# A leftover item's tokens gathered on GpSimd, one register-addressed copy a token

## The chip, the cores and the metric

The kernel runs on one core of one Trainium2 chip. The metric is the device time of one execution in microseconds, as the median over several runs; less is better. A core has five engines that run side by side and wait for each other by semaphores: TensorE (PE, matrix products; PEld is its loading of weights), VectorE (DVE), ScalarE (ACT), GpSimd (POOL) and SyncE (SP, which mostly issues DMAs). Each engine takes its own instructions in order.

## What is computed

Sigmoid attention, then two mixture-of-experts layers. Each of the 1792 tokens (4 batches of 448) has 768 numbers, each layer has 8 experts with 1024 hidden units, and a token uses one expert. Cut to what matters:

```python
x = attention(q, k, v)                                  # 1792 x 768
# layer 1: only tokens with x @ w_skip > 0, the others stay as they are
e_idx = argmax(x @ w_gate, axis=1)
x = x + gate_w * (relu(x @ w1[e_idx]) @ w2[e_idx])      # per token, its own expert
# layer 2: every token
e_idx = argmax(cosine(x, expert_emb) / tau, axis=1)
out = gate_w * (relu(x @ w1[e_idx]) @ w2[e_idx])
```

Everything is in float32. All the weights that are needed come from HBM at run time, since the routing depends on the data.

## The kernel before

The attention takes the first 160 us or so and leaves x transposed in SBUF, as `xT` (128 partitions, 6 chunks of 128 features, 1792 tokens). Most tokens of a batch go to one and the same expert, the primary one. So the kernel computes that expert for the whole batch of 448 tokens (`dense`), and the few tokens that go elsewhere are collected as **items**: an item is up to 64 tokens of one batch that go to one other expert. With these inputs one item is computed in each layer: the first (m = 0) beside the second dense block of layer 1, the other (m = 1) beside the last dense block of layer 2.

`dense` runs over 8 blocks f of 128 hidden units. On TensorE `h(f)` is 18 matmuls (6 chunks, each in three terms of split precision), then come 18 matmuls of `y(f - 1)`; for f = 0 there is no `y` ahead, so `h(0)` is followed directly by `h(1)`. After `h(f)` ACT and DVE evacuate the bank to `hh` and `hl`. Between these pieces are 16 slots, `sub(0)` to `sub(15)`: `sub(2f)` follows `h(f)`, `sub(2f + 1)` follows `y(f - 1)`. A slot emits the work that is hung on it, and since the schedule is manual (`tc.manual_schedule`), that is the order on each engine's queue. In even slots, `units` splits the next weights into a rounded part (ACT) and a remainder (DVE, `split_unit`). In the last block of layer 2, slot 0 first emits `pend`: 24 transposes, the scaling and the store of the output rows of the batch before (`finish`).

What an item hangs on the slots is written in `Item.ready` and `schedule`:

- `regs` loads the item's batch, expert and rank into registers of ACT, DVE and SP; `copy` copies the batch's 6 chunks of `xT` to `STG` (`xT[..., batch]` is addressed by register); both in slot k0, which is 3 for the first item and 1 for the other.
- `select`, four slots later, builds on DVE the selecting matrix `SEL` (token by place in the item, one where they match) and `GRC` (gate and token number).
- `turn(d)`, six of them, transposes a chunk of `STG` to rows in `ROW`, four transposes each, evacuated by ACT.
- `gather` multiplies `SEL` with `ROW` (8 products with 384 columns), `gatherT` turns the gathered rows back with three transposes, into `XB`, which lies in a free part of `ROW`.
- `gate` gathers gates and token numbers by products with `SEL`, and in the first item also transposes `SEL`.
- `first` and `second` fetch the expert's weights into the buffers of the raw weights; `h(s)`, `hT(s)` and `y(s)` compute the item in two halves, `h(0)` in slot 12, `h(1)` in 14; `y` comes after the dense block, in `finish`.
- `put` adds the result into `xT` (first item) or writes its rows to the output by an indirect DMA on GpSimd (the other).

GpSimd otherwise has nothing to do between 38 us and the end.

PSUM banks for this side work come from `bank()`, which alternates between two; dense `h(f)` uses the same two.

Of the kernel before, what the change touches and what calls it, by code (L numbers as in the profile page):

```python
# [12 lines left out]
I32 = mybir.dt.int32  # L13
# [8 lines left out]
def sigmoid_attention_moe_moe_kernel(  # L22
# [645 lines left out]
    def batch_cols(p, b):  # L668
        return xT[:, p, :].rearrange("q (b s) -> q b s", s=S)[:, ds(b, 1), :].rearrange("q o s -> q (o s)")
# [74 lines left out]
    ROW = wp.tile([128, C * DM], F32, tag="row", name="row")  # L744
    SELT = wp.tile([128, S], F32R, tag="selT", name="selT")
    SEL = wp.tile([128, 4 * 128], F32, tag="sel", name="sel")
    XB = ROW[:, 3 * DM : 3 * DM + ND * TL].rearrange("p (c t) -> p c t", t=TL)
    SMALL = wp.tile([128, 16], F32, tag="small", name="small")
    POSC, GS, IDX = SMALL[:P, 0:C], SMALL[:, 12:14], SMALL[:, 14:15].bitcast(I32)
    GRC = SMALL[:P, 4:12].rearrange("p (c t) -> p c t", t=2)  # L750
# [105 lines left out]
    class Item:  # L856


        def __init__(self, m, i):
            self.m, self.i = m, i  # L860
            self.wa, self.wb, self.R = (w1, w2, R1) if m == 0 else (v1, v2, R2)

        def regs(self):
            L, i, xe = self.R.LI, self.i, [ENG.Activation, ENG.DVE]
# [18 lines left out]
                    self.wb[ds(self.e, 1), u * 256 : (u + 1) * 256, :].rearrange("o (g p) d -> p (o g) d", p=128),  # L883
                )

        def copy(self):
            for d in range(ND):
                o = STG[:, d * S : (d + 1) * S]
                if d % 2:
                    nc.vector.tensor_copy(o, batch_cols(d, self.b))  # L890
                else:
                    nc.scalar.activation(o, batch_cols(d, self.b), AF.Copy)

        def select(self):
            R, j = self.R, self.j
            nc.vector.tensor_single_scalar(
# [15 lines left out]
                self.R.LI[0:1, ds(self.i + NL, 1)], engines=[ENG.DVE], min_val=0, max_val=NE - 1  # L912
            )

        def turn(self, d):


            def f():
                ps = bank("ps_xn")
                for c in range(C):  # L920
                    o = d * S + c * P
                    nc.tensor.transpose(ps[:P, c * 128 : (c + 1) * 128], STG[:, o : o + P], ident)
                o = ROW[:P].rearrange("p (c d) -> p c d", c=C)[:, :, d * 128 : (d + 1) * 128]
                nc.scalar.activation(o, ps[:P, :].rearrange("p (c d) -> p c d", c=C), AF.Copy)

            return f

        def gather(self):

            hw = DM // 2  # L930
            ps = bank("ps_xg")
            for c in range(C):
                for g in range(2):
                    nc.tensor.matmul(
                        ps[TL * g : TL * g + TL, :hw], lhsT=SEL[:P, c * 128 : c * 128 + TL],
                        rhs=ROW[:P, c * DM + g * hw : c * DM + g * hw + hw], start=c == 0, stop=c == C - 1,
                    )
            self.xg = spare()
            nc.scalar.activation(self.xg[:, :hw], ps[:, :hw], AF.Copy)

        def gatherT(self):
            ps = bank("ps_xs")
            for i in range(3):
                nc.tensor.transpose(ps[:, i * 128 : i * 128 + 128], self.xg[:, i * 128 : i * 128 + 128], ident)
            nc.scalar.activation(
                XB.rearrange("p (g i) t -> p i g t", g=2), ps[:, :384].rearrange("p (i g t) -> p i g t", i=3, g=2), AF.Copy
            )

        def gate(self):
            ps = bank("ps_gs")  # L950
# [10 lines left out]
        def h(self, s):  # L961


            def f():
                ps = bank("ps_h2")
                for c in range(ND):
                    for g in range(2):
                        nc.tensor.matmul(
                            ps[TL * g : TL * g + TL, :256], lhsT=XB[:, c, :],
                            rhs=as1(QUART[2 * s + g])[:, c, :], start=c == 0, stop=c == ND - 1,  # L970
                        )
                hs = self.hs = spare()
                nc.scalar.activation(hs[:, :256], ps[:, :256], AF.Relu)

            return f
# [37 lines left out]

        def ready(self, k0):

            prep = [self.turn(d) for d in range(ND)] + [self.gather, self.gatherT, self.gate]
            at = merge({k0: [self.regs, self.copy], k0 + 4: self.select}, {5: [lambda: self.first(0)]}, {
                7: [lambda: self.first(1)], 9: [lambda: self.first(2)], 11: [lambda: self.first(3)],
                12: [self.h(0)], 13: [self.hT(0), lambda: self.second(0, 1)],
                14: [self.h(1)], 15: [self.hT(1), lambda: self.second(2, 3)],  # L1020
            })
            return at, prep

        def now(self, hooks=()):

            hooks = list(hooks) + [None] * 3
            self.regs()
            self.first(0, 1, 2, 3)
            self.copy()
            self.select()  # L1030
            for f in self.ready(0)[1]:
                f()
            self.h(0)()
            self.hT(0)()
            self.second(0, 1)
            self.h(1)()
            self.hT(1)()
            self.second(2, 3)
            self.finish(hooks)

        def finish(self, hooks):

            for s in range(2):
                if hooks[s]:
                    hooks[s]()
                self.y(s)
            if hooks[2]:
                hooks[2]()
# [90 lines left out]
    def units1(e):  # L1139
        def f(k):  # L1140
            u, r = k // 4, k % 4
            if r == 0 and u + 2 < NU:
                load_unit(w1, w2, e, u + 2)
            if u + 1 < NU and r % 2 == 0:
                for g in split_unit(u + 1)[:3] if r == 0 else split_unit(u + 1)[3:]:
                    g()

        return f

    def beside(units, steps):  # L1150
# [52 lines left out]
    def block1(j):  # L1203

        b, e = rest_regs(j - 1)
        xs = XST[j % 2]

        def r2():
            if j > 1:
                return {}  # L1210
            f = route2_steps(0, XST[0])
            return at_subs((1, 4, 6, 2, 3, 5, 6, 8), f[:3] + f[6:])

        def general():
            with tc.If(count(R1) > 0) as cmp:
                it = Item(0, 0)
                at, prep = it.ready(3)
                dense(xs, beside(units1(e), schedule(merge(r2(), at), prep, (4, 5, 6, 7, 8, 9, 10, 11, 11))))
                add_y(b)
                it.finish(start2(j > 1))  # L1220
            with cmp.Else():
                dense(xs, beside(units1(e), r2()))
                add_y(b)
                for f in start2(j > 1):
                    f()
                nothing()
            rare()

        def last():
            with tc.If(nc.values_load(R1.LI[0:1, 3 * NL + 3 : 3 * NL + 4], min_val=0, max_val=NL) > 0) as cmp:  # L1230
                it = Item(0, 0)
                at, prep = it.ready(3)
                one, two, three = start2(j > 1)
                steps = schedule(merge({12: one, 14: three}, r2(), at), prep, (4, 5, 6, 7, 8, 9, 10, 11, 11))
                dense(xs, beside(units1(e), steps))
                add_y(b)
                it.finish([two, None, None])
            with cmp.Else():
                general()

        if j == B - 1:
            last()
            return
        with tc.If(NB["n"] > j) as cmp:
# [118 lines left out]
    for j in range(B):  # L1363
# [36 lines left out]
            continue  # L1400
        with tc.If(count(R2) > 0) as cmp:  # L1401
            it = Item(1, 0)
            at, prep = it.ready(1)
            dense(xs, beside(units2, schedule(merge(todo, at), prep, (2, 3, 4, 5, 6, 7, 8, 9, 10))))
            finish(j, b, True)()
            it.finish([None] * 3)
            info = mybir.DependencyInfo(mybir.DependencyClass.Sync, mybir.DependencyReason.DATA)
            tc.add_manual_dep(it.put().ins, STORES[0].ins.name, info, reason="the rows it lands on")
# [40 lines left out]
```

## Time and profile before

| | |
|---|---|
| median of 3 runs | 596.75 us (595.57 to 597.35) |
| the profiled execution | 596.82 us, span from first to last instruction 595.0 us |
| TensorE (PE) busy | 572.8 us, 96% of the span |
| DVE busy | 304.4 us, 51% |
| ACT busy | 275.2 us, 46% |
| GpSimd (POOL) busy | 7.5 us, 1%, in 15 instructions |
| mean granted clock of TensorE | 0.995 of full speed |

The profiled execution is one run; the span leaves out some 2 us of launch and end. The busy share is a share of time in which an instruction runs, not of the peak. For this change the stages count in which an item stands beside a dense block: about 225 to 312 us, and 502 to 586 us.

### The profile page before, as it was taken

How to read it: one execution, taken by the hardware profiler on the slowest of the kernel's cores; microseconds unless marked ns; L12 is line 12 of the kernel's file. 1: busy time of each engine (PE TensorE's matmuls, PEld its weight loads, DVE VectorE, ACT ScalarE, POOL GpSimd, SP SyncE). 2: the span in 40 equal slices, each digit the busy share in tenths (PEclk: the TensorE clock that was granted, in tenths of full speed). 3: DMA queues.
4: the chain of work that ended last, by engine and by line, in shares of the span. 5: the costliest groups of instructions: out<-in, count | busy, mean ns of one | idle time of the engine just before them, and what ended most of it. 6: DMA issues, size and time to landing. Idle time of an engine off the chain costs nothing. (4 is left out here: it accounts for less than half of the span.)

```text
span 595.0 us, 9925 instructions
## 1 busy us (share of the span) xinstructions
PE 572.8 (96%) x3722; PEld 440.0 (74%) x3722; DVE 304.4 (51%) x766; ACT 275.2 (46%) x447; POOL 7.5 (1%) x15
## 2 busy tenths in 40 slices
PE   5999999998999999999999999999999999999993
PEld 3365544534489897987868899979997999898881
DVE  2262435236757778562259664487347663542121
ACT  2676676666932374332138322752256322543020
POOL 2010000000000000000000000000000000000000
PEclk9999999999999999999999999999999999999997
DMA  9978877893460605234545060532317060642433
GB/s 150 117 118 132 109 120 109 122 119 87 166 204 6 209 4 165 103 107 159 188 158 190 2 211 1 188 118 80 133 58 248 1 214 0 223 159 83 159 108 100
DMA packets 139862, 73.31 MB, mean 123 GB/s; under 512 B 103858, under 2 KB 129798, under 8 KB 139792
## 3 DMA queue, kind: packets, MB, share of 16 engines
q1 hardware_dynamic: 116384, 65.94, 41.8%
q10 hardware_dynamic: 23216, 6.43, 6.0%
q8 instruction: 37, 0.61, 0.5%
q14 instruction: 33, 0.27, 0.1%
q0 software_dynamic: 192, 0.07, 0.1%
HBM read 66.90 MB, written 5.70 MB: 122 GB/s over the span
## 5 line engine op out<-in xcount | busy, mean ns | idle before, releaser
L774 PE MATMUL bank<-xs,h 128*128 128x448 f32 x288 | 107.6, 374 | 2.0 <-DVE xT L1165 0.9
L774 PE MATMUL y<-hh,h 128*128 128x448 f32 x288 | 108.5, 377 | 0.0
L794 ACT ACTIVATE hh<-bank 128x448 fp32r<-128x448 f32 x48 | 26.1, 543 | 177.4 <-PE bank L776 166.8
L775 PE MATMUL y<-hl,h 128*128 128x448 f32 x288 | 105.6, 367 | 0.0
L776 PE MATMUL y<-hh,l 128*128 128x448 f32 x288 | 105.6, 367 | 0.0
L776 PE MATMUL bank<-xs,l 128*128 128x448 f32 x288 | 105.3, 365 | 0.3 <-DVE l L765 0.3
L775 PE MATMUL bank<-xs,h 128*128 128x448 f32 x288 | 105.4, 366 | 0.0
L600 ACT ACTIVATE A<-psS,bias 128x896 f32<-128x896 f32 x84 | 83.4, 1006 | 35.9 <-PE psS L596 33.1
L596 PE MATMUL psS<-qT,kT 64*64 64x448 f32 x672 | 88.2, 554 | 0.0
L765 DVE TENSOR_TENSOR l<-r,h 128x512 fp32r<-128x512 f32 (+1 forms) x115 | 85.4, 792 | 4.8 <-ACT h L764 3.0
L795 DVE SCALAR_TENSOR_TENSOR hl<-bank,hh 128x448 fp32r<-128x448 f32 x48 | 29.9, 623 | 113.2 <-ACT hh L794 112.1
L614 PE MATMUL psO<-A,v 64*64 64x448 f32 x672 | 86.4, 539 | 0.0
L764 ACT ACTIVATE h<-r 128x512 fp32r<-128x512 f32 (+1 forms) x115 | 74.6, 710 | 0.0
L774 PEld LDWEIGHTS bank<-xs,h 128*128 128x128 f32 x288 | 54.0, 187 | 11.4 <-DVE hl L795 2.9
L774 PEld LDWEIGHTS y<-hh,h 128*128 128x128 f32 x288 | 54.1, 188 | 8.2 <-issue 2.9
L614 PEld LDWEIGHTS psO<-A,v 64*64 64x64 f32 x672 | 34.8, 133 | 32.3 <-issue 20.2
L776 PEld LDWEIGHTS bank<-xs,l 128*128 128x128 f32 x288 | 54.0, 188 | 5.5 <-DVE l L765 0.6
L776 PEld LDWEIGHTS y<-hh,l 128*128 128x128 f32 x288 | 54.1, 188 | 5.0
L775 PEld LDWEIGHTS y<-hl,h 128*128 128x128 f32 x288 | 54.2, 188 | 4.6 <-issue 0.2
L775 PEld LDWEIGHTS bank<-xs,h 128*128 128x128 f32 x288 | 54.1, 188 | 4.3
L596 PEld LDWEIGHTS psS<-qT,kT 64*64 64x64 f32 x672 | 32.8, 135 | 31.7 <-issue 17.4
L525 DVE COPY xT<-psO 64x448 f32<-64x448 f32 x24 | 14.9, 621 | 48.0 <-PE psO L614 47.7
(251 smaller groups left out, 452.8 us busy)
## 6 DMA issues: line engine op xcount, KB each, us to landing
r<-in_moe_w_dram SPq DMA_DIRECT2D x62, 768.0 KB, 5.9
v<-in_v_dram ACTq DMA_DIRECT2D x48, 112.0 KB, 3.6
k<-in_k_dram SPq DMA_DIRECT2D x44, 112.0 KB, 3.6
q<-in_q_dram SPq DMA_DIRECT2D x44, 112.0 KB, 4.0
out_dram<-row SPq DMA_DIRECT2D x3, 1344.0 KB, 6.9
out_dram<-row SPq DMA_DIRECT2D x1, 896.0 KB, 5.5
stg<-in_moe_w_dram SPq DMA_DIRECT2D x1, 768.0 KB, 6.4
row<-in_moe_w_dram SPq DMA_DIRECT2D x1, 768.0 KB, 8.2
```

The costliest lines, as they stand in the source:

```text
L525: nc.vector.tensor_copy(x, ps[64 * j : 64 * j + 64, :S])
L596: nc.tensor.matmul(ps[KT * i : KT * i + KT, j, :S], lhsT=kT[r, i, h * KT : (h + 1) * KT], rhs=qT[r, i], start=True, stop=True,)
L600: nc.scalar.activation(at, ps[:, :, :S], AF.Sigmoid, bias=bias, scale=1.0 / math.sqrt(D))
L614: nc.tensor.matmul(ST[w, "o"][i][D * j : D * j + D, :S], lhsT=t[r, j, h, :], rhs=at[r, j, :], start=h == 0, stop=h == NH - 1,)
L764: nc.scalar.activation(dst_h, src, AF.Copy)
L765: nc.vector.tensor_sub(dst_l, src, dst_h.bitcast(F32))
L774: nc.tensor.matmul(ps, lhsT=ah, rhs=bh, start=first, stop=False)
L775: nc.tensor.matmul(ps, lhsT=ah, rhs=bl, start=False, stop=False)
L776: nc.tensor.matmul(ps, lhsT=al, rhs=bh, start=False, stop=last)
L794: nc.scalar.activation(a, ps[:, :S], AF.Relu)
L795: nc.vector.scalar_tensor_tensor(l, ps[:, :S], 0.0, a.bitcast(F32), op0=ALU.max, op1=ALU.subtract)
```

## The change

The item's tokens are no longer taken out by transposing the whole batch and multiplying with the selecting matrix. Instead `places` computes, with four small products of the token numbers (`GRC[:, c, 1:2]`, a weight of one column) with `SEL`, the column of `xT` in which each of the 64 places has its token; DVE adds the offset, clamps it to a valid column and writes it into one row of 64 integers (`places_`). Then `gather` runs over the 64 places on GpSimd: load the number into a register, and copy that column of all six chunks, 128 partitions by 6 elements, from `xT` to `xb`. Places without a token copy a clamped column, and their gate is zero. `copy`, `turn`, the old `gather` and `gatherT` go. The buffers move: `xb` and `places_` lie in `ROW` for the first item and in `STG` for the other.

The slots change too: `regs` and `select` both stand in slot 0, `places` and `gather` in slot 1, `gate` in 6; `h(0)` moves from slot 12 to 13, `h(1)` from 14 to 15, and `hT(1)` to the beginning of `Item.finish`, behind the dense block. `places` flips the bank counter once, so that it takes the bank that `h` took last.

```diff
+            home = (ROW, STG)[m]
+            self.xb = home[:, 3 * DM : 3 * DM + ND * TL].rearrange("p (c t) -> p c t", t=TL)
+            self.places_ = home[0:1, 2 * DM : 2 * DM + TL].bitcast(I32)
...
-        def turn(self, d):
+        def places(self):
+
+            turn[0] ^= 1
+            ps = bank("ps_pl")
+            for c in range(C):
+                nc.tensor.matmul(
+                    ps[0:1, :TL], lhsT=GRC[:, c, 1:2], rhs=SEL[:P, c * 128 : c * 128 + TL], start=c == 0, stop=c == C - 1
+                )
+            nc.vector.tensor_scalar(self.places_, ps[0:1, :TL], float(SKIP), float(NT - 1), op0=ALU.add, op1=ALU.min)
+
+        def gather(self, t0, t1):
...
             def f():
-                ps = bank("ps_xn")
-                for c in range(C):
-                    o = d * S + c * P
-                    nc.tensor.transpose(ps[:P, c * 128 : (c + 1) * 128], STG[:, o : o + P], ident)
-                o = ROW[:P].rearrange("p (c d) -> p c d", c=C)[:, :, d * 128 : (d + 1) * 128]
-                nc.scalar.activation(o, ps[:P, :].rearrange("p (c d) -> p c d", c=C), AF.Copy)
+                for t in range(t0, t1):
+                    o = nc.values_load(self.places_[0:1, t : t + 1], engines=[ENG.Pool], min_val=0, max_val=NT - 1,
+                                       skip_runtime_bounds_check_because="places() clamps it to 0 .. NT - 1")
+                    nc.gpsimd.tensor_copy(self.xb[:, :, t : t + 1], xT[:, :, ds(o, 1)])
...
-            prep = [self.turn(d) for d in range(ND)] + [self.gather, self.gatherT, self.gate]
-            at = merge({k0: [self.regs, self.copy], k0 + 4: self.select}, {5: [lambda: self.first(0)]}, {
+            prep = [self.places, self.gather(0, TL), self.gate]
+            at = merge({k0: [self.regs, self.select]}, {5: [lambda: self.first(0)]}, {
                 7: [lambda: self.first(1)], 9: [lambda: self.first(2)], 11: [lambda: self.first(3)],
-                12: [self.h(0)], 13: [self.hT(0), lambda: self.second(0, 1)],
-                14: [self.h(1)], 15: [self.hT(1), lambda: self.second(2, 3)],
+                13: [self.h(0)], 14: [self.hT(0), lambda: self.second(0, 1)],
+                15: [self.h(1), lambda: self.second(2, 3)],
             })
...
-                at, prep = it.ready(3)
+                at, prep = it.ready(0)
                 one, two, three = start2(j > 1)
-                steps = schedule(merge({12: one, 14: three}, r2(), at), prep, (4, 5, 6, 7, 8, 9, 10, 11, 11))
+                steps = schedule(merge({12: one, 14: three}, r2(), at), prep, (1, 1, 6))
...
-            at, prep = it.ready(1)
-            dense(xs, beside(units2, schedule(merge(todo, at), prep, (2, 3, 4, 5, 6, 7, 8, 9, 10))))
+            at, prep = it.ready(0)
+            dense(xs, beside(units2, schedule(merge(todo, at), prep, (1, 1, 6))))
```

How the order of instructions changes, at three places. Line numbers of the changed kernel are its own.

TensorE in the dense block of the first item, the end of `h(0)` and the start of `h(1)`. Before:

```order
L774 MATMUL bank_1696<-xs_94,h_1704 128x448
L775 MATMUL bank_1696<-xs_94,h_1704 128x448
L776 MATMUL bank_1696<-xs_94,l_1705 128x448
L774 MATMUL bank_1697<-xs_94,h_1704 128x448
L775 MATMUL bank_1697<-xs_94,h_1704 128x448
```

After (`L914` is `places`, `sel` and `small` are `SEL` and the tile that holds `GRC`):

```order
L773 MATMUL bank_1696<-xs_94,h_1704 128x448
L774 MATMUL bank_1696<-xs_94,h_1704 128x448
L775 MATMUL bank_1696<-xs_94,l_1705 128x448
L914 MATMUL bank_1696<-sel,small 1x64 x4
L773 MATMUL bank_1697<-xs_94,h_1704 128x448
```

The four small products now stand between the two blocks, and they read `SEL`.

DVE in the same place, from the evacuation of `h(0)` (`hl`) to that of `h(1)`. Before:

```order
L795 SCALAR_TENSOR_TENSOR hl_77<-bank_1696,hh_75 128x448
L765 TENSOR_TENSOR l_1709<-r_91,h_1708 128x512 x3
L1079 TENSOR_LOAD pb
L676 ISA
L676 TENSOR_TENSOR xs_93<-xT,xs_93 128x448
L676 ISA
L676 TENSOR_TENSOR xs_93<-xT,xs_93 128x448
L795 SCALAR_TENSOR_TENSOR hl_78<-bank_1697,hh_76 128x448
```

After (`TENSOR_LOAD` loads a register, `ISA` computes with registers, `L899` writes `SEL`):

```order
L794 SCALAR_TENSOR_TENSOR hl_77<-bank_1696,hh_75 128x448
L764 TENSOR_TENSOR l_1709<-r_91,h_1708 128x512 x3
L867 TENSOR_LOAD LI_104
L869 TENSOR_LOAD LI_104
L869 ISA x2
L905 TENSOR_LOAD LI_104
L905 ISA x2
L890 ISA
L890 TENSOR_SCALAR small<-POS_97 112x4
L894 ISA
L894 TENSOR_TENSOR small<-small,kcol 112x4
```

The register loads and `select` moved to here, behind the splits of the weights (`l`); the masks (`L899 TENSOR_SCALAR sel`) come two instructions further on.

TensorE in the dense block of the other item, the end of `pend` (`stg` is `STG`, `y` the banks it is turned into) and the start of `h(1)`. Before:

```order
L1326 MATMUL y_1698<-ident,stg 112x128 x4
L1326 MATMUL y_1699<-ident,stg 112x128 x2
L774 MATMUL bank_1697<-xs_94,h_1704 128x448
L775 MATMUL bank_1697<-xs_94,h_1704 128x448
L776 MATMUL bank_1697<-xs_94,l_1705 128x448
```

After:

```order
L1306 MATMUL y_1698<-ident,stg 112x128 x4
L1306 MATMUL y_1699<-ident,stg 112x128 x2
L914 MATMUL bank_1696<-sel,small 1x64 x4
L773 MATMUL bank_1697<-xs_94,h_1704 128x448
L774 MATMUL bank_1697<-xs_94,h_1704 128x448
```

Here `places` stands behind the transposes of `pend`, and DVE's queue has, ahead of `select`, the scaling of the output rows as well as the splits.

## Rows read from the trace of the kernel before

**Rows 1.** Busy us by stage (PE, PEld, DVE, ACT, POOL), granted clock, DMA share, GB/s.

```profile
225.00:300.00 75.00, 74.96 (x422) 63.59 (x423) 38.88 (x96) 25.11 (x48) 0.00 (x0) 1.00 0.43 144
```

**Rows 2.** Timeline of TensorE, first item: start us, length, engine, line, instruction.

```profile
228.78 0.37 PE L774 MATMUL bank<-xs,h 128*128 128x448 f32 x1
...
251.10 0.60 PE L922 MATMUL bank<-ident,stg 128*112 128x128 f32 x4
251.45 0.45 PE L774 MATMUL y<-hh,h 128*128 128x448 f32 x1
...
267.68 2.80 PE L934 MATMUL bank<-row,sel 112*64 112x384 f32 x16
270.41 0.47 PE L774 MATMUL y<-hh,h 128*128 128x448 f32 x1
...
274.16 0.49 PE L944 MATMUL bank<-ident,xg 128*128 128x128 f32 x3
274.49 0.95 PE L952 MATMUL bank<-small,sel 112*128 112x2 f32 x8
```

**Rows 3.** Timeline of TensorE, second item.

```profile
508.46 0.45 PE L774 MATMUL bank<-xs,h 128*128 128x448 f32 x1
...
517.29 0.65 PE L922 MATMUL bank<-ident,stg 128*112 128x128 f32 x4 [0.75 <-DVE hl L795]
```

**Rows 4.** Timeline of TensorE, small products with one-column weights.

```profile
497.65 0.83 PE L450 MATMUL bank<-pm,pc 128*1 128x64 f32 x12
```

**Rows 5.** Timeline of DVE, first item.

```profile
231.33 1.89 DVE L765 TENSOR_TENSOR l<-r,h 128x512 fp32r<-128x512 f32 x3
...
259.65 0.17 DVE L896 TENSOR_SCALAR small<-POS 112x4 f32 x1 [0.73 <-issue]
...
260.06 0.87 DVE L905 TENSOR_SCALAR sel<-io,small 112x128 f32<-112x128 f32 x4
```

**Rows 6.** Register work of DVE by line, first item: ns min/median/max, first and last start.

```profile
L1079 DVEq TENSOR_LOAD <-pb x1: 317/317/317, 231.2 to 231.2; - x1
...
L865 DVEq TENSOR_LOAD <-LI x1: 305/305/305, 240.1 to 240.1; - x1
...
L867 DVEq SEQ_ASSERT  x1: 35/35/35, 241.2 to 241.2; - x1
...
L911 DVEq TENSOR_LOAD <-LI x1: 311/311/311, 258.7 to 258.7; - x1
```

**Rows 7.** The same, second item, and the output store under way then.

```profile
L865 DVEq TENSOR_LOAD <-LI x1: 1187/1187/1187, 510.8 to 510.8; - x1
...
L1355 SPq DMA_DIRECT2D out_dram<-row x1: 358/358/358, 509.6 to 509.6; - x1
...
DMA to landing us min/median/max: 6.9/6.9/6.9
```

**Rows 8.** Busy time and clock at the end; one matmul line early and later.

```profile
585.60:588.90 3.30, 0.06 (x2) 0.00 (x0) 0.62 (x1) 0.00 (x0) 0.00 (x0) 1.00 0.29 88
589.10:595.00 5.90, 0.00 (x0) 0.00 (x0) 0.00 (x0) 0.00 (x0) 1.08 (x1) 0.50 0.05 8
...
L596 PE MATMUL psS<-qT,kT x24: 654/947/1006, 14.2 to 18.7; 64*64 64x448 f32 x24
...
L596 PE MATMUL psS<-qT,kT x36: 536/536/724, 18.6 to 25.0; 64*64 64x448 f32 x36
```

**Rows 9.** GpSimd: a register load, and a small operation over 128 partitions.

```profile
L1230 POOLq TENSOR_LOAD <-LI x1: 293/293/293, 221.4 to 221.4; - x1
...
L100 POOL IOTA io_i<- x1: 253/253/253, 4.5 to 4.5; 128x128 int32 x1
```

**Rows 10.** Timeline of TensorE, the first `h` of each item.

```profile
279.51 2.81 PE L968 MATMUL bank<-r,row 128*64 128x256 f32 x24
...
556.74 2.81 PE L968 MATMUL bank<-r,row 128*64 128x256 f32 x24
```

**Rows 11.** The item's second weights, last two requests of the first item, to landing.

```profile
DMA to landing us min/median/max: 4.5/5.5/6.6
```

More of the change, by code (lines that the diff above doesn't have):

```diff
@@ L746, in sigmoid_attention_moe_moe_kernel @@
     SEL = wp.tile([128, 4 * 128], F32, tag="sel", name="sel")
-    XB = ROW[:, 3 * DM : 3 * DM + ND * TL].rearrange("p (c t) -> p c t", t=TL)
     SMALL = wp.tile([128, 16], F32, tag="small", name="small")
@@ L884, in second @@
                 )
[L886 to L892, printed above, removed]
         def select(self):
@@ L913, in e_dve @@
             )
-        def turn(self, d):
-            def f():
-                ps = bank("ps_xn")
-                for c in range(C):
-                    o = d * S + c * P
-                    nc.tensor.transpose(ps[:P, c * 128 : (c + 1) * 128], STG[:, o : o + P], ident)
-                o = ROW[:P].rearrange("p (c d) -> p c d", c=C)[:, :, d * 128 : (d + 1) * 128]
-                nc.scalar.activation(o, ps[:P, :].rearrange("p (c d) -> p c d", c=C), AF.Copy)
-            return f
[L928 to L947, printed above, removed]
+        def places(self):
[7 more added lines that the diff above has]
+        def gather(self, t0, t1):
+            def f():
+                for t in range(t0, t1):
+                    o = nc.values_load(self.places_[0:1, t : t + 1], engines=[ENG.Pool], min_val=0, max_val=NT - 1,
+                                       skip_runtime_bounds_check_because="places() clamps it to 0 .. NT - 1")
+                    nc.gpsimd.tensor_copy(self.xb[:, :, t : t + 1], xT[:, :, ds(o, 1)])
+            return f
         def gate(self):
@@ L968, in f @@
                         nc.tensor.matmul(
-                            ps[TL * g : TL * g + TL, :256], lhsT=XB[:, c, :],
+                            ps[TL * g : TL * g + TL, :256], lhsT=self.xb[:, c, :],
                             rhs=as1(QUART[2 * s + g])[:, c, :], start=c == 0, stop=c == ND - 1,
@@ L1028, in now @@
             self.first(0, 1, 2, 3)
-            self.copy()
             self.select()
@@ L1036, in now @@
             self.h(1)()
-            self.hT(1)()
             self.second(2, 3)
@@ L1041, in finish @@
         def finish(self, hooks):
+            self.hT(1)()
             for s in range(2):
@@ L1216, in general @@
                 it = Item(0, 0)
-                at, prep = it.ready(3)
-                dense(xs, beside(units1(e), schedule(merge(r2(), at), prep, (4, 5, 6, 7, 8, 9, 10, 11, 11))))
+                at, prep = it.ready(0)
+                dense(xs, beside(units1(e), schedule(merge(r2(), at), prep, (1, 1, 6))))
                 add_y(b)
@@ L1231, in last @@
                 it = Item(0, 0)
-                at, prep = it.ready(3)
+                at, prep = it.ready(0)
                 one, two, three = start2(j > 1)
-                steps = schedule(merge({12: one, 14: three}, r2(), at), prep, (4, 5, 6, 7, 8, 9, 10, 11, 11))
+                steps = schedule(merge({12: one, 14: three}, r2(), at), prep, (1, 1, 6))
                 dense(xs, beside(units1(e), steps))
@@ L1402, in sigmoid_attention_moe_moe_kernel @@
             it = Item(1, 0)
-            at, prep = it.ready(1)
-            dense(xs, beside(units2, schedule(merge(todo, at), prep, (2, 3, 4, 5, 6, 7, 8, 9, 10))))
+            at, prep = it.ready(0)
+            dense(xs, beside(units2, schedule(merge(todo, at), prep, (1, 1, 6))))
             finish(j, b, True)()
```

## The prediction

> **What bounds the kernel now.** I read the page's busy table first, then the busy time by stage, then the timelines around the two items (an item is up to 64 leftover tokens of one expert). In the stage that holds the first item, 225 to 300 us, TensorE is busy for 74.96 of 75 us at a granted clock of 1.00, VectorE for 38.88 and GpSimd for none [rows 1]; around the second item the matmuls follow each other as closely [rows 3]. So in these stages a microsecond taken off TensorE is a microsecond of the span, and a microsecond for which TensorE waits is one too. The profiled execution took 596.82 us for a span of 595.0, and the median of the runs is 596.75: I add changes of the span to 596.8.
>
> **What leaves TensorE.** A group of four turn transposes starts at 251.10, and the next dense matmul at 251.45: 0.35 us. There are six groups an item: 2.1 us. The selecting product runs from 267.68 until the next dense matmul at 270.41: 2.7 us. The three transposes of what it gathered run from 274.16 until the gate product follows at 274.49: 0.33 us [rows 2]. Together 5.15 us an item, 10.3 for the two. The copies and evacuations that ACT and DVE lose (six copies and eight evacuations an item) lie beside TensorE's work and are worth nothing by themselves, with one exception: in the second item the transposes at 517.29 waited 0.75 us for DVE [rows 3], whose queue had been held up by register loads between two evacuations. The loads now come earlier, and this 0.75 goes.
>
> **What TensorE gets.** `places` is four products of a one-column weight with 64 columns. The nearest row has this shape: 12 such instructions (six products) take 0.83 us [rows 4], so four cost 0.55 us. The gate, `h`, `hT` and `y` are the same work in another slot.
>
> **The wait that is added.** This term decides the sign. `places` reads SEL, which DVE's `select` writes. Before, `select` ran four slots after the register loads, and SEL was written by 260.9 and first read by the selecting product at 267.68 [rows 2, 5]. Now the register loads and `select` stand in slot 0 and `places` in slot 1. In the first block there is no `y` of an earlier block between these slots, so on TensorE nothing stands between the end of `h(0)` and `places`, and behind `places` is queued the whole of `h(1)`, for which ACT and DVE wait in turn. What DVE has to do once `h(0)` has ended:
>
> First item. TensorE is free at 228.78 [rows 2]. DVE evacuates `h(0)`; the three splits of the next weights start at 231.33 and take 1.89, to 233.22 [rows 5]. A register load that stands behind the splits in DVE's queue was issued at 231.2 already [rows 6], so loads lie beside them. The loads that stand there now cost what the same lines cost before: from 240.1 (first load) to 241.2 (the assertion behind the second), 1.13 us, and from the third load at 258.7 to the first operation of `select` at 259.65, 0.91 us [rows 5, 6]. So 231.2 + 2.04 = 233.2, just as the splits end. `select` lasts from 259.65 to the end of its masks at 260.06 + 0.87: 1.28 us [rows 5]. SEL is there at 234.5; with a tenth for the signal TensorE waits **5.8 us**.
>
> Second item. Slot 0 also holds the 24 transposes of the previous batch, after which `h(1)` started at 508.46 [rows 3]. The first register load behind the splits is issued at 510.8 and takes 1187 ns, where the same line took 305 in the first item [rows 6, 7]: an output store is under way, issued at 509.6 and landed 6.9 us later [rows 7]. I take three such loads, 0.88 us more each than in the first item: 510.8 + 2.04 + 2.64 + 1.28 = 516.8, so TensorE waits **8.3 us**. Lower bound, loads as in the first item: 5.7. Upper bound, the third load only done when the store has landed at 516.5, with 0.6 of register work and 1.28 behind it: 9.9.
>
> Sum without the clock. First item: -5.15 + 0.55 + 5.8 = +1.2. Second: -5.15 - 0.75 + 0.55 + 8.3 = +2.95. Together +4.15, which gives 601.0.
>
> **The clock.** No wait in the middle of the trace is as long as these. At the end TensorE stopped at about 585.7; the granted clock was 1.00 up to 588.9 and is 0.50 from 589.1 on, so it fell after 3.3 us without work [rows 8]. Both new waits are longer, so I let the clock fall to 1.2 GHz in both. What coming back costs has one pair of rows: in the attention the same matmul takes 947 ns (median) in those from 14.2 us on and 536 ns in those from 18.6 on [rows 8], so some 4.5 us ran at half speed and lost 2.25. Twice that is 4.5, and the sum is +8.65: **605**. Bounds: nothing, and 4.5 a wait (I double the row, because TensorE had run slow transposes ahead of it too). The Trainium skill says in "TensorE: Matmul & The Clock Gate", section "What's actually happening", that the throttled state is the default and activity releases it; the rows at both ends agree, and none shows a fall in mid-kernel.
>
> **What GpSimd gets, and what hides it.** 64 tokens, each a register load, an address computation and a copy of 128x6. GpSimd's load took 293 ns [rows 9]; no copy of this kind is in the trace. Lower bound, the rest beside the next load: 0.3 us a token, 19 us. Upper bound, all in series: 0.29, address work like the 0.3 between the end of a third load and `select` (half of 0.6) [rows 5, 6], and a copy like GpSimd's 128x128 iota, 0.25 [rows 9]: 0.84 us, 54 us. What covers it is dense matmul work up to the item's first `h`. In the first item that stood at 279.51 [rows 10]; less 5.15, plus 0.55, 5.8, 2.25 of slow clock, and 3.75 because it moves from slot 12 to 13, behind one more block (270.41 to 274.16 [rows 2]): 286.7. The places are stored by about 236.5 (SEL, the products, and two split operations of 0.63 ahead in DVE's queue), so 50 us are there, 0.78 a token. In the second item, from 517.6 to 556.74 [rows 10] - 5.15 - 0.75 + 0.55 + 8.3 + 2.25 + 3.75 = 565.7: 0.75 a token. I take 0.5 to 0.6, between the bounds, since load and address work are the terms with rows, and cost the gather at nothing; each 0.1 us a token above 0.75 costs some 6 us an item.
>
> **Other moves.** `h(1)` now stands in slot 15, so the second half of the item's weights is requested one block later. It landed 4.5 and 6.6 us after issue [rows 11]; behind `h(1)` stand a block of 3.75 and the first half of the item's `y` before it is read. I cost it at nothing; without that half of `y` it would be 2.9 us. The first weights are requested in the same slots as before.
>
> **The rivals.**
> A. The clock stays up, or falls in one wait only: 601.0 to 603.2. For it: the one fall in the trace is in an idle end. Against: both waits are well over its 3.3 us. Chance 0.15.
> B. The wait is short, and the kernel becomes **faster**: if TensorE found SEL ready, 596.8 - 10.3 - 0.75 + 1.1 = 586.9. The two waits together decide: at 9.95 us, with the clock kept, the change is worth nothing. I have 14.1, and for less the loads and `select` would have to run while `h(0)` still runs. In the queue they stand behind splits that wait for ACT, which waits for `h(0)`. Chance 0.07.
> C. The gather comes late. Above 0.75 us a token TensorE also waits in slot 13; at 0.84 it is 4 and 6 us, with two further falls of the clock 605 + 10 + 4.5 = 620. Chance 0.15; by the rows alone I would have said a tenth. The Trainium skill ("GPSIMD Engine Reference", section "Specifications") has GpSimd and VectorE share their SBUF interfaces, with contention when DVE has two SBUF inputs, as the splits have; no run here shows it yet, and it raises this chance. The same page ("Performance pitfalls for Q7 kernels") charges some 102 cycles for each small read command; as an estimate that is 0.085 us a copy at its 1.2 GHz, and the copies would stay hidden.
> D. The sum comes within 0.3% (1.8 us) of before, say by waits of 4 and 7 us and no fall: 0.05.
>
> **How the numbers follow.** The forecast, two waits with two falls, has 0.58 and gives 605 (602 to 609 on its own). The range goes down to 599 to hold A, with somewhat shorter waits, and up to 612 for the longer waits, the dearer clock and the beginning of C; outside are B, D and the far part of C, under 0.2. About 0.3% is what a measurement of this kernel can tell from no change. Faster: B, 0.07. Same: D and a little of A, 0.07. Slower: 0.86.
>
> **What would show it.** In the profile after, the `places` matmuls should have 5 to 6 us and 8 to 9 us of idle time before them, released by DVE's masks; the dense matmuls behind them should follow at some 0.4 us instead of 0.2 for a few microseconds, with a granted clock of 0.5; the turn transposes and the selecting product are gone, and no more than 1 us stands before the item's first `h`. If `h` waits for GpSimd, C is right; if `places` waits under 5 us in either item, my queue argument is wrong; if the clock stays at 1.00, A.

## The result, and the profile after

The changed kernel takes 603.16 us (median of 4 runs, 601.88 to 603.91), the kernel before in the same comparison 596.88 us: a ratio of 1.0107 with a 95% interval of 1.0083 to 1.013, so **slower by some 6.3 us**. 605.0 was predicted. The profiled execution of after took 603.18 us for a span of 601.1 us, with a mean granted clock of 0.979.

The page's busy times of after:

```profile
PE 567.3 (94%) x3652; PEld 436.4 (73%) x3652; DVE 302.5 (50%) x762; ACT 263.4 (44%) x425; POOL 41.9 (7%) x143
```

The change does what it says: GpSimd's busy time goes from 7.5 to 41.9 us, TensorE's falls by 5.5 us (and would have fallen further, had some of its work not run at half clock), ACT's by 11.8. And yet the span is 6.1 us longer. Of TensorE's waits, the two longest that before's list doesn't have (us in all, how many, the longest):

```profile
PE bank L914 <- DVE sel L899: 13.6, 2, 8.2
...
PE bank L773 <- ACT xs L834: 1.8, 1, 1.8
```

The first row is the wait that the prediction is about, 13.6 us in two pieces; the second is one that it does not have. TensorE's timeline in the first item, which answers to [rows 2]:

```profile
228.94 0.37 PE L775 MATMUL bank<-xs,l 128*128 128x448 f32 x1
234.72 1.01 PE L914 MATMUL bank<-sel,small 112*1 112x64 f32 x8 [5.41 <-DVE sel L899]
235.66 0.74 PE L773 MATMUL bank<-xs,h 128*128 128x448 f32 x1
236.20 0.57 PE L774 MATMUL bank<-xs,h 128*128 128x448 f32 x1
...
238.86 0.37 PE L773 MATMUL bank<-xs,h 128*128 128x448 f32 x1
```

and in the second item, which answers to [rows 3]:

```profile
509.74 2.78 PE L1306 MATMUL y<-ident,stg 128*112 128x128 f32 x24
520.72 1.01 PE L914 MATMUL bank<-sel,small 112*1 112x64 f32 x8 [8.20 <-DVE sel L899]
521.66 0.74 PE L773 MATMUL bank<-xs,h 128*128 128x448 f32 x1
522.20 0.57 PE L774 MATMUL bank<-xs,h 128*128 128x448 f32 x1
...
525.18 0.37 PE L773 MATMUL bank<-xs,h 128*128 128x448 f32 x1
```

L914 is `places`. Nothing of the dense `h(1)` passes it: TensorE stands still for 5.41 and 8.20 us. The rows behind it tell the second half of the story: the matmul that takes 0.37 us a few microseconds later takes 0.57 here. The stretches of TensorE's work at and behind `places` (columns as in [rows 1], the granted clock is the 1.00 or 0.50):

```profile
234.72:238.40 3.68, 3.68 (x15) 2.92 (x16) 1.72 (x6) 0.00 (x0) 0.53 (x3) 0.50 0.71 220
238.50:300.00 61.50, 61.50 (x342) 52.92 (x341) 25.80 (x74) 16.32 (x31) 16.50 (x61) 1.00 0.35 117
...
520.72:525.10 4.38, 4.38 (x17) 3.53 (x18) 0.74 (x4) 0.00 (x0) 1.17 (x6) 0.50 1.06 382
525.20:530.00 4.80, 4.80 (x25) 4.40 (x24) 2.03 (x3) 2.02 (x3) 2.77 (x9) 1.00 0.14 47
```

So the clock fell to the lower of its levels, 1.2 GHz, in both waits, and TensorE worked 3.7 and 4.4 us at half speed before it was back. Half of that, 1.8 and 2.2 us, is an upper estimate of the loss, since `places` is in part paced by DVE's masks at either clock (run 8).

Why SEL is late in the first item stands in DVE's timeline of after:

```profile
225.80 4.91 DVE L1056 TENSOR_REDUCE G<-row 128x448 f32<-128x2688 f32 x1
231.63 0.62 DVE L794 SCALAR_TENSOR_TENSOR hl<-bank,hh 128x448 fp32r<-128x448 f32 x1 [0.92 <-ACT h L763]
232.17 1.89 DVE L764 TENSOR_TENSOR l<-r,h 128x512 fp32r<-128x512 f32 x3
233.97 0.16 DVE L890 TENSOR_SCALAR small<-POS 112x4 f32 x1
```

TensorE's `h(0)` has ended at 229.31, but DVE is in a sum of squares for the routing (`G`) until 230.71 and evacuates the bank only at 231.63, behind ACT. Then come the splits, and `select` (L890) starts as they end: the three register loads lie beside them. In the second item the same timeline shows a gap:

```profile
513.58 1.90 DVE L764 TENSOR_TENSOR l<-r,h 128x512 fp32r<-128x512 f32 x3 [0.29 <-ACT h L763]
519.97 0.17 DVE L890 TENSOR_SCALAR small<-POS 112x4 f32 x1 [4.49 <-issue]
...
520.38 0.87 DVE L899 TENSOR_SCALAR sel<-io,small 112x128 f32<-112x128 f32 x4
```

And its register loads there, which answer to [rows 7] (ns min/median/max, first and last start):

```profile
L867 DVEq TENSOR_LOAD <-LI x1: 1202/1202/1202, 514.6 to 514.6; - x1
...
L869 DVEq TENSOR_LOAD <-LI x1: 1205/1205/1205, 515.9 to 515.9; - x1
...
L905 DVEq TENSOR_LOAD <-LI x1: 1822/1822/1822, 517.6 to 517.6; - x1
```

DVE computes nothing for 4.49 us between the splits and `select`, and in this time its queue does three loads that take 1.2, 1.2 and 1.8 us. In the first item the same three take 0.30 to 0.31 us each. The gather on GpSimd in after, in the first item the register loads and the copies, in the second the copies:

```profile
L924 POOLq TENSOR_LOAD <-row x64: 284/286/298, 236.5 to 267.1; - x64
...
L926 POOL COPY row<-xT x64: 188/195/936, 237.3 to 267.5; 128x6 f32 x64
...
L926 POOL COPY stg<-xT x64: 188/194/1006, 522.6 to 552.6; 128x6 f32 x64
```

The first `h` of each item in TensorE's timeline of after, which answers to [rows 10]:

```profile
285.60 0.65 PE L949 MATMUL bank<-r,row 128*64 128x256 f32 x4
...
568.63 0.87 PE L949 MATMUL bank<-r,stg 128*64 128x256 f32 x6
```

The gather takes 30.4 us in the first item (237.3 to 267.7), 0.47 to 0.48 us a token, and ends 18 and 15 us before `h` reads it. This is how the 6.1 us of span divide by stages, from the first dense matmul of a stage to the first of the next:

| stage | before | after | difference |
|---|---|---|---|
| up to the first item's dense block | 225.04 | 225.40 | +0.36 |
| first item's dense block, to the item's `y` | 75.40 | 77.48 | +2.08 |
| the item's `y`, and the end of its `If` | 5.99 | 7.22 | +1.23 |
| layer 2 up to the last dense block | 195.82 | 195.96 | +0.14 |
| second item's dense block, to the output transposes | 75.32 | 79.53 | +4.21 |
| the end | 17.46 | 15.53 | -1.93 |

The first and the last row aren't the theory's. In the first lies a stretch of the attention, 146.4 to 149.6 us, in which the clock is at 0.50 in after and at 1.00 in before, behind a wait of 2.05 us (2.06 in before). The end lasts 15.0 to 15.9 us in all ten traces with the gather on GpSimd (after and the nine runs below), and 17.5 in the one trace of before.

### The profile page after: what moved, and what is told of

It is laid out like the page before. It is cut to its first block, busy times and chain, and to the rows that moved or that the text cites. A ratio compares the mean times of both kernels' runs of the same rounds, so it can differ in the third digit from the quotient of the medians.

```text
span 601.1 us, 10123 instructions
## 1 busy us (share of the span) xinstructions
PE 567.3 (94%) x3652; PEld 436.4 (73%) x3652; DVE 302.5 (50%) x762; ACT 263.4 (44%) x425; POOL 41.9 (7%) x143
## 5 line engine op out<-in xcount | busy, mean ns | idle before, releaser
L773 PE MATMUL bank<-xs,h 128*128 128x448 f32 x288 | 108.6, 377 | 2.6 <-ACT xs L834 1.8
L774 PE MATMUL bank<-xs,h 128*128 128x448 f32 x288 | 106.6, 370 | 0.2 <-issue 0.2
L773 PEld LDWEIGHTS bank<-xs,h 128*128 128x128 f32 x288 | 54.9, 191 | 13.4 <-DVE hl L794 2.9
L774 PEld LDWEIGHTS bank<-xs,h 128*128 128x128 f32 x288 | 55.0, 191 | 4.4
```

The costliest lines, as they stand in the source:

```text
L773: nc.tensor.matmul(ps, lhsT=ah, rhs=bh, start=first, stop=False)
L774: nc.tensor.matmul(ps, lhsT=ah, rhs=bl, start=False, stop=False)
```

## The experiments

**The theory**: the loss is the wait for SEL in each item, because registers, masks and `places` stand in neighbouring slots, plus the clock that falls in it. **Rivals**: the gather on GpSimd costs the time (by coming late or by getting in DVE's way); or the clock costs nothing of its own.

**1. `places` and the gather two slots later, in both items.**

```diff
-                dense(xs, beside(units1(e), schedule(merge(r2(), at), prep, (1, 1, 6))))
+                dense(xs, beside(units1(e), schedule(merge(r2(), at), prep, (3, 3, 6))))
...
-            dense(xs, beside(units2, schedule(merge(todo, at), prep, (1, 1, 6))))
+            dense(xs, beside(units2, schedule(merge(todo, at), prep, (3, 3, 6))))
```

> The changed kernel with places and gather hung on slot 3 instead of 1, in both items; nothing else moves. Theory (the wait of places for SEL, and the slow clock behind it, are the whole loss): in the first item the wait of 5.4 us and some 1.8 us of half speed go; in the second 8.2 and 2.1 go, but about 2 us of wait stay, since the evacuation of the block before stands behind select on DVE there: 603.2 - 15.5 + 2.2 = about 588 to 590, faster than before by over 1%. Rival (what costs is GpSimd's copying beside DVE, or the later slots of h): the wait goes, but something else in the same stage takes its place, and the time stays above 597.

589.41 us, ratio to before 0.9881 (0.9852 to 0.991), as the theory has it. The slot alone is worth 603.16 - 589.41 = 13.75 us and turns the loss into a gain; the gather is the same. What is left of the wait at `places`, in this kernel's list of waits:

```profile
PE bank L914 <- DVE hl L794: 1.7, 1, 1.7
```

And the stretch of the second item a microsecond behind it:

```profile
514.80:518.10 3.30, 3.30 (x10) 2.95 (x9) 0.71 (x2) 0.00 (x0) 0.90 (x5) 0.50 1.07 373
```

Even this wait, of 1.7 us, was followed by half clock.

**2. The same in the first item alone.**

> The changed kernel with places and gather on slot 3 in the first item alone; the second item keeps slot 1. Theory: 5.4 us of wait and 1.8 of half speed go in the first item and the second keeps its 8.2 us wait: about 596. Rival (the items are not independent, or only the second one costs): 600 to 603.

597.79 us, ratio 1.0011 (0.9994 to 1.0029): between the two, nearer to the theory. The second item keeps its wait of 8.2 us. Against before, the first item's block is 4.7 us shorter in this run's trace and the second's 5.0 longer: the second alone eats all that the change gives.

**3. The waits filled with work.** Transposes into an unused bank ahead of `places`, so that TensorE has something to do:

```diff
+            if BANKS:
+                for i in range(84 if self.m else 52):
+                    nc.tensor.transpose(BANKS[turn[0] ^ 1][:, i % 4 * 128 : i % 4 * 128 + 128], ident, ident)
```

> The changed kernel with TensorE kept at work ahead of places: 52 transposes of the identity in the first item, 84 in the second, into the bank that h(1) overwrites afterwards; some 4.6 and 7.4 us of work inside waits of 5.4 and 8.2. Theory (the fall of the clock is paid on top of the waits): the granted clock stays at 1.00 through both, and 1.8 + 2.1 us come back: about 599.3. Rival (the clock's part is nothing, since the stages have slack behind the wait): 603, and slower than that if the transposes do not fit.

609.38 us, ratio 1.0217 (1.0187 to 1.0247): expected 599.3, missed. TensorE's timeline in the first item:

```profile
231.59 0.71 PE L773 MATMUL bank<-xs,h 128*128 128x448 f32 x1 [5.92 <-DVE G L1059]
...
237.37 5.84 PE L913 MATMUL bank<-ident 128*128 128x128 f32 x52
243.14 0.61 PE L917 MATMUL bank<-sel,small 112*1 112x64 f32 x8
```

Here the block's own first `h(0)` waited 5.92 us for DVE, with a fall of the clock (why it waits in this kernel isn't known); the transposes then came on top of a wait that had already passed. The first item tells nothing. In the second the 84 transposes took 9.33 us, longer than the wait, and yet the dense block lasted 78.39 us, 1.1 less than in after, at a clock of 1.00: a sign for the theory, with a cost of its own mixed in. Run 8 repeats the test in the second alone.

**4. One token gathered in place of 64** (the other 63 columns are left out).

```diff
-            prep = [self.places, self.gather(0, TL), self.gate]
+            prep = [self.places, self.gather(0, 1), self.gate]
```

> The changed kernel with one token gathered in place of 64, so the item's other 63 columns are whatever lay there and the output differs. Theory (GpSimd's work is hidden: copies end some 18 and 16 us ahead of the first h, and DVE is not slowed): 603 within 1 us. Rival (GpSimd beside DVE costs, by the shared SBUF interface): 1 to 4 us faster.

602.18 us, ratio 1.0092 (1.006 to 1.0123). 63 loads and copies in each item are worth at most 1 us, within what two comparisons can differ by. DVE's splits of the larger weights from 238 to 267 us, where the gather lies, in after (count, busy us, mean ns, idle):

```profile
L764 DVE TENSOR_TENSOR l<-r,h 128x768 fp32r<-128x768 f32 x4 | 3.7, 956 | 0.2
```

The same with one token:

```profile
L764 DVE TENSOR_TENSOR l<-r,h 128x768 fp32r<-128x768 f32 x4 | 3.7, 957 | 0.2
```

956 and 957 ns: the copies don't slow them. It is the copies that wait. GpSimd's copies and DVE's splits in after:

```profile
242.39 2.15 POOL L926 COPY row<-xT 128x6 f32 x5 [0.28 <-issue]
...
242.27 1.83 DVE L764 TENSOR_TENSOR l<-r,h 128x768 fp32r<-128x768 f32 x2
```

The first two of these five copies last 0.89 and 0.94 us, the others 0.19. In after, 21 of the 128 copies last 0.45 us or more; each of them ran into a DVE instruction `l` or `xs`, which have two SBUF inputs, and ended within 0.06 us of its end, and no copy got through inside one. The rule of the Trainium skill ("GPSIMD Engine Reference", section "Specifications") of contention with DVE instructions of two SBUF inputs, which had raised the chance of rival C, is thus seen here, on GpSimd's side alone. It costs this kernel nothing: the loads run on during a held copy, the short copies behind it catch up, and the gather ends 15 us early all the same.

**5. `hT(1)` of the first item ahead of the additions of `y`.** This is for the +1.23 us at the end of the first item, which no step of the prediction has. The queue of TensorE reaches the branch that ends the item's `If` later than before, and the branch takes as long as ever. Before (ns, start):

```profile
L1230 PEldq COMPARE_BRANCH  x1: 3662/3662/3662, 302.6 to 302.6; - x1
```

After:

```profile
L1210 PEldq COMPARE_BRANCH  x1: 3822/3822/3822, 306.1 to 306.1; - x1
```

In after the branch ends only at 309.9, when the item's matmuls have been done since 308.25. It starts 3.2 us behind the start of the item's `y`, where before it was 2.2: `y` needs the SEL of `hT(1)`, whose transposes stand right ahead of `y` now, and whose copy on DVE stands behind six additions (DVE's timeline of after), so that SEL is there only 0.85 us after `y` has begun:

```profile
299.79 3.59 DVE L1145 TENSOR_TENSOR xT<-xT,y 128x448 f32 x6 [4.06 <-PE y L775]
303.30 0.42 DVE L963 COPY sel<-bank 128x256 f32<-128x256 f32 x1
```

```diff
                 dense(xs, beside(units1(e), schedule(merge(r2(), at), prep, (1, 1, 6))))
+                it.hT(1)()
+                it.turned = True
                 add_y(b)
```

> The changed kernel with hT(1) of the first item put ahead of add_y, so that its evacuation to SEL does not stand behind six additions on DVE. Theory: behind the dense block TensorE's sequencer gets to the branch that ends the item some 3.5 us earlier, its 3.8 us branch is again hidden behind the item's y, and the 1.84 us of idle time ahead of the next h falls to about 0.6: 1.2 us less than the changed kernel, 602. Rival (the 1.84 us is a wait for ACT's halves, as the trace puts it down): no difference, 603.2.

603.78 us, ratio 1.0121 (1.01 to 1.0142): nothing gained, missed. The idle time at the branch fell from 1.84 to 0.67 us, but the copy is now ahead of the additions, and the item's `y` waits for those (this kernel's list of waits):

```profile
PE y L973 <- DVE xT L1146: 1.0, 1, 1.0
```

The wait moved on the same queue (and `places` waited 6.26 us for SEL in the first item of this execution, 0.85 more than in after, which the edit doesn't touch). The additions had delayed the copy by only some 0.3 us: it starts 0.42 us behind the start of its transposes here and 0.74 in after. The rest is the late place of the transposes: in run 7, where `hT(1)` is back in its slot ahead of the end of the block, the branch starts 2.1 us behind `y` and 0.49 us of idle time are left.

**6 and 9. The output store kept away from the register loads.** Run 6 holds the store of the next to last batch back to slot 3 of the last block, on SP; run 9 issues it from ACT there:

```diff
-            nc.sync.dma_start(
+            def store(queue=nc.sync, bq=b):
+                queue.dma_start(
...
+                todo = merge({3: lambda: HELD[-1](nc.scalar, bl)}, todo)
```

> The changed kernel with the output store of the batch before issued in slot 3 of the last block instead of right behind its scaling. Theory (the register loads are slow because that store is under way): the three loads take some 0.3 us each, and the second wait shrinks from 8.2 to about 5.6 us: 600.6. Rival (the loads are slow from weight loads, or for another reason): they stay at 1.2 us, and the time at 603.

> As the changed kernel, but the output store of the next to last batch is issued by ACT, in slot 3 of the last dense block, behind the evacuation of h(1), instead of by SP as soon as its rows are scaled: so it cannot be under way while DVE loads the item's three registers. Theory (the loads of 1.2 to 1.8 us are slow because an output store is under way): the three loads take about 0.3 us each, the wait of places in the second item falls from 8.2 to about 5.5 us as in the first item, and the kernel takes 603.2 - 2.7 = 600.5 (599.5 to 601.5). The clock still falls in the shorter wait, as in the first item. Rival (something else in this place makes them slow, say the weights that stream in): the loads stay at 1.2 us and more, the wait at 8.2, the time at 603.2.

Run 6 gave 603.62 us, ratio 1.0106 (1.0078 to 1.0134), and tested nothing: SP is ahead of the compute engines and reached the store at 513.9 us all the same; the loads still took 1.05 to 1.53 us. Run 9 gave **600.49 us**, ratio 1.0068 (1.0049 to 1.0086). Its three loads and its store (ns, first and last start):

```profile
L867 DVEq TENSOR_LOAD <-LI x1: 315/315/315, 517.4 to 517.4; - x1
...
L869 DVEq TENSOR_LOAD <-LI x1: 302/302/302, 517.8 to 517.8; - x1
...
L905 DVEq TENSOR_LOAD <-LI x1: 304/304/304, 518.5 to 518.5; - x1
...
L1336 ACTq DMA_DIRECT2D out_dram<-row x1: 384/384/384, 526.5 to 526.5; - x1
```

And `places` in its timeline of TensorE:

```profile
520.15 1.00 PE L914 MATMUL bank<-sel,small 112*1 112x64 f32 x8 [4.89 <-DVE sel L899]
```

Without a store under way a load takes 0.3 us, and the wait falls from 8.20 to 4.89. By itself this doesn't part the store from the weights, since no DMA at all moved data from 517.2 to 519.0 us in this run. But the slowness went with the store: it now fell on GpSimd's gather, three of whose 64 loads took over 1 us just behind 526.5 (the longest is the third of the three durations):

```profile
L924 POOLq TENSOR_LOAD <-stg x64: 284/285/1145, 521.4 to 553.7; - x64
```

And in after, where the store has landed at 520.3, the weights that stream in at 382 GB/s behind it (the stretch from 520.72 us above) slow none of the 64 loads:

```profile
L924 POOLq TENSOR_LOAD <-stg x64: 284/285/297, 522.0 to 551.9; - x64
```

**8. The second item's wait filled with work.** As in run 3, with 72 transposes, in the second item alone.

> As the changed kernel, but in the second item alone 72 further TensorE transposes into an unused bank stand ahead of places: at the 0.111 us each that such transposes took in the earlier run they last about 8.0 us, so they fill the wait of 8.2 us for SEL and leave some 0.2 of it. The first item is as in the changed kernel. Theory (part of the loss in the second item is the clock that falls in the wait, not only the wait): the granted clock stays at 1.00 through the second item, the matmuls behind places follow at their usual pace, and about 2.2 us come back: 603.2 - 2.2 = 601.0 (600 to 602). Rival (the slow matmuls behind the wait cost nothing, because something else than the clock sets their pace): 603.2, within 0.5.

Its timeline of TensorE:

```profile
513.14 8.02 PE L913 MATMUL bank<-ident 128*128 128x128 f32 x72
521.45 0.86 PE L917 MATMUL bank<-sel,small 112*1 112x64 f32 x8 [0.29 <-DVE sel L899]
522.24 0.47 PE L773 MATMUL bank<-xs,h 128*128 128x448 f32 x1
522.55 0.37 PE L774 MATMUL bank<-xs,h 128*128 128x448 f32 x1
```

And the stretch behind the wait:

```profile
521.40:525.80 4.40, 4.35 (x25) 3.64 (x26) 0.79 (x4) 0.00 (x0) 1.18 (x6) 1.00 1.05 381
```

`places` comes as late as in after, 8.15 us behind the end of the last matmul of use (8.20 there); the only thing that differs is what TensorE did meanwhile, and now the clock is 1.00 and the matmuls behind take 0.37. From the start of `places`, its four products and the next nine matmuls take 2.7 us here and 4.5 in after. The dense block lasts 77.65 us in place of 79.53: the clock alone costs **1.7 to 1.9 us** in this item. (In the five traces that leave this wait as it is, those of after and runs 2, 4, 5 and 6, the block lasts 79.0 to 80.4 us.) The whole kernel took 602.2 us (601.77 to 603.43), ratio 1.0104 (1.0086 to 1.0122), just above what I expected; of the 1.9 us, its profiled run lost 1.2 in layer 2, where the clock fell behind the branch's idle time, as it had not in after's. The verdict rests on the block; the times of the whole don't settle 1.9 us.

**7. A version without the waits.** The first item as in run 1; in the second the registers and `select` ahead of the dense block, `places` in slot 1 as before; `h` and `hT` in their old slots.

```diff
             at, prep = it.ready(0)
+            for f in at.pop(0):
+                f()
             dense(xs, beside(units2, schedule(merge(todo, at), prep, (1, 1, 6))))
...
-                13: [self.h(0)], 14: [self.hT(0), lambda: self.second(0, 1)],
-                15: [self.h(1), lambda: self.second(2, 3)],
+                12: [self.h(0)], 13: [self.hT(0), lambda: self.second(0, 1)],
+                14: [self.h(1)], 15: [self.hT(1), lambda: self.second(2, 3)],
```

> The gather on GpSimd without the waits: first item with places and gather on slot 3, second item with regs and select emitted ahead of the dense block and places on slot 1, and h and hT back in slots 12 to 15. Theory: no wait of places above 0.5 us in either item, the clock at 1.00, the gather done well before slot 12; the removed 5.15 us an item and 0.75 are then gained: 596.9 - 10.3 - 0.75 + 1.2 = 587, perhaps 585. Rival (an item's TensorE work was not worth its full length, for instance since h now waits for GpSimd or for weights): 590 to 596.

**584.32 us**, ratio 0.979 (0.9764 to 0.9815), 12.9 us faster than before. The stretch of the second item in which after waits:

```profile
500.00:530.00 30.00, 30.00 (x168) 27.61 (x167) 13.24 (x28) 10.43 (x18) 10.73 (x40) 1.00 0.59 191
```

TensorE is busy in all of its 30 us at a clock of 1.00, with the gather beside it. The three loads of `regs` and `select` stand ahead of the store here (at 500.4 to 501.5 us; the store is issued at 506.5) and take 0.30 to 0.32 us.

## Why the prediction was right

**The two waits** were 5.41 and 8.20 us, predicted 5.8 and 8.3. The step from queue to wait held: DVE reaches `select` behind the splits and the loads, and TensorE has nothing else. The second, longer wait rests on loads slowed by a store, and runs 9 and 7, with the gather's loads in after, show that it is the store: without it, loads of 0.3 us. The sums are closer than their terms, and in the second item that is luck, since two errors cancel. From the first load to `select` it took 5.34 us in the second item where I had 4.68, since I gave the third load the 1.2 us of the first [rows 7] and it took 1.8 (the trace of before had the better row: a third load in this place, of another line, took 1.71 us at 513.8); in both items `places` began 0.75 us after `select` did, not 1.28, since its first product needs the first mask and not all four.

**The clock** fell in both waits, and cost at most 1.8 us in the first item (half of the 3.7 us at half speed; no run takes it apart there) and 1.7 to 1.9 in the second (run 8), predicted 2.25 each. Rival A, with one fall or none, is ruled out by the granted clock of both stretches. The fall from which I concluded, at the end of before's trace, came after 3.3 us without work; in run 1 the clock was at half behind a wait of 1.7 us already.

**What left TensorE** was mis-sized, in the kernel's favour. In run 7 the second item's block is 69.37 us against 75.32: 5.95 us net of `places`, where my terms give 5.15 + 0.75 - 0.55 = 5.35. In run 1 the first item's block is 70.30 without a wait of 0.36, against 75.40: 5.1, where I had 4.6. The rows tell what I most likely left out: behind each small group the next dense matmul takes 0.45 to 0.47 us, not 0.37 [rows 2], and with six groups and a product gone this is 0.08 to 0.1 seven times, 0.6 to 0.7 us.

With the measured terms the blocks close: -5.1 + 5.41 + 1.8 = +2.1 (measured +2.08), and -5.95 + 8.20 + 1.7 to 1.9 = +3.95 to +4.15 (measured +4.21). I had +3.45 and +5.2.

**The gather** took 0.47 to 0.48 us a token, below the 0.5 to 0.6 that I took and well inside the 0.75 that were there, and hid completely (run 4). The bound from both sides, with the load as the term that has a row, was the right one; rival C falls, though the contention that had raised its chance is there. A copy that nothing held up took 0.19 us, where the estimate in rival C was 0.085.

**What I did not have**: moving `hT(1)` to the beginning of `Item.finish` puts its transposes right ahead of the item's `y`, and its copy behind the additions in DVE's queue. I costed the move of `h(1)` by its weights alone, and took `hT` for the same work in another slot: 1.23 us. And the end came 1.93 us sooner: TensorE ended 8.1 and 8.3 us behind the start of the output transposes, and the rest, which is mostly stores landing, took 9.4 and 7.2 us. All ten traces with the gather agree on it, so it isn't chance in after; but there is one trace of before, and the cause stays open. So the span's measured +6.1 against the predicted +8.65 is -1.0 and -1.4 in the second and first block, +1.2 at the branch, -1.9 at the end, and +0.5 elsewhere: the sign and the two large terms were worked out, while the end, which no step has, is the largest single difference.

**Rival B** tells what the change could have been worth: for its 586.9, with SEL ready when TensorE comes, the kernel needs other slots, and run 1 comes within 2.5 us of it and run 7 passes it by 2.6.

## What to carry to other kernels

Work handed to an idle engine is free only from the slot in which its inputs are ready: write down, for the first instruction of the chain on the bound engine, what every engine ahead of it has in its queue at that moment, and put two slots of other work between if it isn't enough. A wait of 5 to 8 us on TensorE cost nearly 2 us more in clock, so price the matmuls behind each new wait too. Load registers before an output store is issued, not behind it, and when a step moves to right ahead of the work that needs it, follow its copy on the other engine too.

## What the runs showed of the hardware

- A register load takes 0.28 to 0.32 us in the rows above, and up to 1.2 to 1.8 us in the 6 us behind the issue of an output store. In all eleven traces every load over 0.9 us lies there, on whichever engine. Weights that stream in don't do it: while they came at 382 GB/s (after, 520.7 to 525.1 us), with no store under way, GpSimd's loads took 285 to 294 ns.
- A copy on GpSimd that runs into a DVE instruction with two SBUF inputs lasts until that instruction ends: 0.45 to 1.0 us in place of 0.19 in after, while the DVE instruction takes 956 ns beside such copies and 957 without.
- The branch at the end of the first item's `If` took TensorE's sequencer 3.3 to 3.8 us in the eleven traces. It costs the span only what of it isn't covered by matmuls already queued: TensorE is idle for 0.61 us before, 1.84 after. The Trainium skill ("Runtime: NRT & Kernel Launch", section "Instruction fetch mechanics") says that a taken branch out of the fetched pages forces a fetch before execution goes on. The traces agree as far as they go: in all eleven, a 16 KB packet of a queue for instructions starts 0.9 to 1.5 us into this branch, where the whole of before has 37 of them in 595 us. Which engine a packet is for, they don't say.
- The clock falls in mid-kernel too. Here it did with waits of 5.41, 8.20, 4.89 and 1.7 us. With idle times of about 2 us it did in some executions and not in others: at the branch in runs 8 and 9 (1.89 and 2.18 us), not in after (1.84); in the attention in after (2.05), not in before (2.06).
